# Gate rows by column matmuls and DMA, projections spread over slots, tiles finished at even steps

## The chip, the cores and the metric

One core of a Trainium2 chip. The metric is the device time of one execution in microseconds, median over runs. Where the times of two kernels are compared, the runs come from the same chip in the same rounds, unless the text says otherwise.

## The reference, cut to what matters

An adaptive layer norm, attention with 32 query heads over 8 groups of keys, a gated residual, a second norm, a spatial gating MLP, a second gated residual. Only the lines that the change touches:

```python
mod = (_silu(c) @ w_mod).reshape(c.shape[0], 6, 1, -1)
sa, ca, ga, sb, cb, gb = (mod[:, 0].copy(), ..., mod[:, 5].copy())   # cut
h = _layernorm(x, axis=-1) * (1 + ca) + sa
x = x + ga * _A_ref(h, A_k_cache, A_v_cache, A_wq, A_wo)             # ga: gate row 1
h = _layernorm(x, axis=-1) * (1 + cb) + sb
x = x + gb * _B_ref(h, B_w_in, B_w_sp, B_b_sp, B_w_out)              # gb: gate row 2
```

`x` is 2048 x 512, `c` one row of 512. `ga` and `gb` are needed as rows, the same on all 128 partitions.

## The kernel before

The attention runs as 128 iterations of 8 slots. A slot has a score pair (two 512-column matmuls into one of two `s_ps` buffers), one exponential on ScalarE, eight matmuls of probabilities by values of the iteration before (P.V), and whatever `fill` and `at` put there: query projections for later iterations, output projections, norms. `(it, i)` is iteration and slot; what `at` adds runs ahead of the slot's score pair, what `fill` adds runs after its P.V matmuls.

```python
def mod_part(i, wmod, w0, mc_ps):              # 16 matmuls of one column
    for dt in range(NDT):
        for kt in range(NDT):
            nc.tensor.matmul(mc_ps[:, i * NDT + dt : i * NDT + dt + 1],
                lhsT=wmod[:, kt, w0 + dt * P : w0 + (dt + 1) * P],
                rhs=sc_bf[:, kt : kt + 1], start=(kt == 0), stop=(kt == NDT - 1))

def ln1_turn(j0, n, xns):                      # transposes, then modulation; cut
    for half in range(2):
        t_ps = bank("misc")[:].bitcast(BF16).rearrange("p (k q) -> p k q", k=2)
        ...                                    # 2*n transposes into t_ps
        ...                                    # VectorE: two modulations out of t_ps

at(0, 3, first_turn)                           # turns tile 1
at(0, 6, lambda: ln1_turn(2, 2, first["x2"]))  # turns tiles 2 and 3: 8 transposes
...
fill[0, 4] = qproj(0, list(range(REP)), P, P)  # 16 projections of tile 1, then one copy
rest_q = qproj(0, [0, 1], 2 * P, 2 * P) + qproj(0, [2, 3], 2 * P, 2 * P)
fill[0, 7], fill[1, 0], fill[1, 1] = rest_q[0:5], rest_q[5:11], rest_q[11:16]
...
# the last column of the MLP: seven gate steps of 128 columns
for f in range(NFT):                           # NFT = 7
    spatial(last, yT, f, n_a, P, bias_by_pe=True)      # 16 matmuls, bias, VectorE multiply
    ...                                                # output matmuls of step f - 1
    if f % 2 == 1:
        finish_tile(last, f // 2, o2_last[f // 2])     # two VectorE operations, a store
```

`bank("misc")` hands out two PSUM banks (buffers that matmuls write their results into) in turn: the transposes of `ln1_turn`, the projections and the output projections all take theirs from these two. `bank("o_ps")` has two banks of its own.

## Time and profile before

| | before |
|---|---|
| time, first three runs | 1322.39 us (1322.29 to 1322.67) |
| span of the trace | 1320.8 us |
| TensorE busy | 1301.5 us (99%) |
| ScalarE busy | 1076.7 us (82%) |
| first score pair starts | 10.65 us |
| first slot with the next chunk's projections | its score pair at 31.42 us |
| last operation before the last store starts | 1316.08 us |

Read the table with the chain of waits in mind, the profile's list that goes back from the last instruction, at each step to what released it: TensorE carries 98% of it. Something is won only where TensorE has less to execute or waits less. The last three rows are landmarks.

### The profile page before, as it was taken

How to read it: one execution, taken by the hardware profiler on the slowest of the kernel's cores; microseconds unless marked ns; L12 is line 12 of the kernel's file. 1: busy time of each engine (PE TensorE's matmuls, PEld its weight loads, DVE VectorE, ACT ScalarE, POOL GpSimd, SP SyncE). 2: the span in 40 equal slices, each digit the busy share in tenths (PEclk: the TensorE clock that was granted, in tenths of full speed). 3: DMA queues.
4: the chain of work that ended last, by engine and by line, in shares of the span. 5: the costliest groups of instructions: out<-in, count | busy, mean ns of one | idle time of the engine just before them, and what ended most of it. 6: DMA issues, size and time to landing. Idle time of an engine off the chain costs nothing.

```text
span 1320.8 us, 27675 instructions
## 1 busy us (share of the span) xinstructions
PE 1301.5 (99%) x12130; PEld 858.3 (65%) x12335; DVE 473.4 (36%) x1166; ACT 1076.7 (82%) x1061; POOL 49.2 (4%) x92
## 2 busy tenths in 40 slices
PE   9999999999999999999999999999999999999998
PEld 5666666666666666666666666666666666644445
DVE  6532222222222222222222222222222566784444
ACT  7898999999999999999999999999999999650000
POOL 1200000000000000000000000000000000020000
PEclk9999999999999999999999999999999999999999
DMA  7541022102111122111210221021101111153300
GB/s 180 148 97 33 16 47 37 37 17 49 31 24 37 30 37 37 33 34 37 33 37 13 53 37 33 18 53 23 31 14 21 25 31 31 34 116 80 69 21 26
DMA packets 148720, 58.12 MB, mean 44 GB/s; under 512 B 138384, under 2 KB 144784, under 8 KB 148592
## 3 DMA queue, kind: packets, MB, share of 16 engines
q1 hardware_dynamic: 141792, 37.65, 15.4%
q0 software_dynamic: 4208, 16.39, 4.2%
q10 hardware_dynamic: 2592, 2.23, 0.5%
q8 instruction: 98, 1.61, 0.5%
q14 instruction: 30, 0.25, 0.1%
HBM read 21.37 MB, written 2.10 MB: 18 GB/s over the span
## 4 chain that ended last, share of the span: by engine, by line
PE 98%; issue 1%; DMA 0%; DVE 0%; ACT 0%; SPq 0%; DVEq 0%
PE s_ps L972 36%; PE o_ps L994 35%; PE misc L939 7%; PE misc L1345 7%; PE misc L1026 6%; PE s_ps L1191 2%; PE s_ps L1230 2%; PE o_ps L1366 1%; PE s_ps L1366 0%; DMA wmod_a<-in_w_mod_dram 0%; PE misc L1102 0%; DVE tmp L1378 0%; DVE yout L1379 0%; PE misc L849 0%; PE misc L1353 0%
## 5 line engine op out<-in xcount | busy, mean ns | idle before, releaser
L979 ACT ACTIVATE pT<-s_ps 128x1024 bf16<-128x1024 f32 x1024 | 1043.4, 1024 | 83.4 <-PE s_ps L972 8.5
L994 PEld LDWEIGHTS <-pT 128*128 128x128 bf16 x8192 | 548.5, 98 | 241.2
L994 PE MATMUL o_ps<-v,pT 128*128 128x129 bf16 x8192 | 631.4, 220 | 0.0
L972 PE MATMUL s_ps<-qT,kT 128*128 128x512 bf16 x2048 | 609.0, 379 | 10.0 <-ACT pT L979 0.2
L1005 DVE RECIPROCAL rall<-o_ps 128x2 f32<-128x2 f32 x256 | 43.7, 171 | 744.1 <-PE o_ps L994 744.0
L972 PEld LDWEIGHTS <-kT 128*128 128x128 bf16 x2048 | 199.3, 98 | 119.5 <-issue 1.0
L939 PE MATMUL misc<-hT,wq_g 128*128 128x512 bf16 (+2 forms) x466 | 166.4, 370 | 0.1
L1026 PE MATMUL misc<-wo_g,oT 128*128 128x512 bf16 x386 | 146.3, 379 | 0.0
L1006 DVE TENSOR_TENSOR onorm<-o_ps,rall 128x256 bf16<-128x256 f32 x256 | 108.6, 424 | 9.0 <-DVE rall L1005 0.3
L1345 PE MATMUL misc<-wsp,z 128*128 128x512 bf16 (+2 forms) x555 | 100.5, 336 | 0.6 <-issue 0.3
L950 DVE CAST qT<-misc 128x512 bf16<-128x512 f32 x127 | 86.4, 680 | 1.9 <-PE misc L939 1.6
L1345 PEld LDWEIGHTS <-z 128*128 128x128 bf16 x560 | 50.6, 98 | 48.5
L1039 DVE TENSOR_TENSOR xacc<-misc,xacc 128x512 f32<-128x512 f32 x112 | 76.2, 680 | 0.0
L939 PEld LDWEIGHTS <-wq_g 128*128 128x128 bf16 x528 | 50.5, 98 | 0.7
L1026 PEld LDWEIGHTS <-oT 128*128 128x128 bf16 x512 | 50.1, 98 | 0.8
L1360 DVE TENSOR_TENSOR gb<-misc,bsp_bc 128x512 bf16<-128x512 f32 (+1 forms) x28 | 18.4, 658 | 58.6 <-PE misc L1345 58.6
L1191 PE MATMUL s_ps<-win_sb,hT 128*128 128x448 bf16 x128 | 27.0, 352 | 0.1
L1201 ACT ACTIVATE z<-s_ps 128x896 bf16<-128x896 f32 x16 | 14.7, 917 | 14.9 <-PE s_ps L1191 14.9
L1230 PE MATMUL s_ps<-hT,win_sb 128*128 128x512 bf16 x109 | 24.3, 379 | 0.2
L1238 ACT ACTIVATE z1T<-s_ps 128x1024 bf16<-128x1024 f32 x14 | 14.3, 1023 | 10.1 <-PE s_ps L1230 9.1
L691 DVE BATCH_NORM_STATS2 bnst<-x_sb 128x6 f32<-128x512 bf16 x32 | 21.9, 683 | 1.3 <-DMA x_sb<-in_A_x_dram 0.8
L715 POOL DMA_DIRECT2D wq_g<-in_A_wq_dram x7 | 5.2, 750 | 420.9 <-PE misc L939 420.9
(87 smaller groups left out, 281.5 us busy)
## 6 DMA issues: line engine op xcount, KB each, us to landing
wq_g<-in_A_wq_dram POOLq DMA_DIRECT2D x7, 512.0 KB, 4.0
v<-in_A_v_cache_dram POOLq DMA_DIRECT2D x7, 512.0 KB, 7.3
wo_g<-in_A_wo_dram POOLq DMA_DIRECT2D x7, 512.0 KB, 4.7
oT<-onorm SPq DMA_TRANSPOSE x128, 2.4
wsp<-in_w_mod_dram POOLq DMA_DIRECT2D x1, 2048.0 KB, 11.1
out_dram<-yout ACTq DMA_DIRECT2D x16, 128.0 KB, 1.7
win_sb<-in_B_w_in_dram POOLq DMA_DIRECT2D x1, 1792.0 KB, 7.6
x_sb<-in_A_x_dram SPq DMA_DIRECT2D x3, 512.0 KB, 5.9
```

The source lines that it names most:

```text
L939: nc.tensor.matmul(ps[0][:, o0 : o0 + n], lhsT=wqs[g][:, dt, hh * DH : (hh + 1) * DH], rhs=hTs[ch][:, dt, c0 : c0 + n], start=(dt == 0), s ...
L950: nc.vector.tensor_copy(out=dst, in_=src)
L972: nc.tensor.matmul(s_ps[:, h * 512 : (h + 1) * 512].rearrange("p (r q) -> p r q", r=REP), lhsT=groups[g]["kT"][:, kt * P : (kt + 1) * P], ...
L979: nc.scalar.activation(out=pTs[u][:, 2 * i : 2 * i + 2, :], in_=s_ps[:].rearrange("p (k q) -> p k q", k=2), func=ACT.Exp, scale=inv_sqrt_dh,)
L994: nc.tensor.matmul(o_ps[:, hh % 2, 0 : DH + 1], lhsT=pTs[u][:, kt, hh * P : (hh + 1) * P], rhs=groups[g]["v1"][:, kt, 0 : DH + 1], start=( ...
L1005: nc.vector.reciprocal(out=rall[:, c0 : c0 + 2], in_=o_ps[:, :, DH])
L1006: nc.vector.tensor_tensor(out=onorms[u][:, hh - 1 : hh + 1, :], in0=o_ps[:, :, 0:DH], in1=rall[:, c0 : c0 + 2].unsqueeze(2).to_broadcast([ ...
L1026: nc.tensor.matmul(X_ps[:], lhsT=oTs[u][:, hh, :], rhs=groups[g]["wo"][:, hh, :], start=(hh == 0), stop=(hh == REP - 1),)
L1039: nc.vector.tensor_tensor(out=xaccs[j][:], in0=X_ps[:], in1=xaccs[j][:], op=ALU.add)
L1191: nc.tensor.matmul(ps[0][:, hf * 512 : hf * 512 + FC], lhsT=h2Ts[j // CT][:, dt, (j % CT) * P : (j % CT + 1) * P], rhs=win_sb[:, dt, FH + ...
L1230: nc.tensor.matmul(ps[0][:, k * 512 : (k + 1) * 512], lhsT=win_sb[:, dt, f * P : (f + 1) * P], rhs=h2Ts[2 * ch2 + k][:, dt, :], start=(dt ...
L1345: nc.tensor.matmul(g_ps[:, :n], lhsT=z2[:, st, f * P : (f + 1) * P], rhs=wsp[t][:, st, c0 : c0 + n], start=(st == 0), stop=(st == NT - 1 a ...
```

## The change

The intent has three parts. The gate rows are computed as columns (cheap one-column matmuls) and turned into rows by a trip through DRAM, in place of eight 512-column matmuls. The projections near the start are spread thinner, so that ScalarE should not wait for score pairs behind long runs of projections. And three of the last four tiles are finished one gate step earlier.

```diff
-    def mod_row(row_out, i, lhs):
-        mr_ps = bank("misc")
-        for kt in range(NDT):
-            nc.tensor.matmul(mr_ps[:], lhsT=lhs[kt][:], rhs=wmod_b[:, kt, ...], ...)   # cut
-        nc.vector.tensor_copy(out=row_out[:], in_=mr_ps[:])
+    def mod_rows():
+        mc_ps = bank("misc")
+        for i, row in enumerate((0, 3)):
+            mod_part(i, wmod_b, row * D, mc_ps)
+        for i, (part, rows) in enumerate(((2, ga_rows), (5, gb_rows))):
+            cols = slice(part * NDT, (part + 1) * NDT)
+            nc.vector.tensor_copy(out=modc[:, cols], in_=mc_ps[:, i * NDT : (i + 1) * NDT])
+            line = dram.tile([D], FP32, name=f"mod{part}")
+            nc.gpsimd.dma_start(out=line[:].rearrange("(dt p) -> p dt", p=P), in_=modc[:, cols])
+            nc.gpsimd.dma_start(out=rows[:], in_=line[:].partition_broadcast(P))
...
-    fill[0, 4] = qproj(0, list(range(REP)), P, P)
+    next_q = qproj(0, list(range(REP)), P, P)
+    fill[0, 4], fill[0, 5] = next_q[0:8], next_q[8:16]
     rest_q = qproj(0, [0, 1], 2 * P, 2 * P) + qproj(0, [2, 3], 2 * P, 2 * P)
-    fill[0, 7], fill[1, 0], fill[1, 1] = rest_q[0:5], rest_q[5:11], rest_q[11:16]
+    fill[0, 7] = rest_q[0:4]
+    for i in range(6):
+        fill[1, i] = rest_q[4 + 2 * i : 6 + 2 * i]
...
-    at(10, 4, lambda: mod_row(ga_rows, 2, rest_w["lhs"]))
-    at(11, 4, lambda: mod_row(gb_rows, 5, rest_w["lhs"]))
+    at(10, 4, mod_rows)
...
-        if f % 2 == 1:
+        if f % 2 == 0 and f < 2 * (CT - 1):
             finish_tile(last, f // 2, o2_last[f // 2])
```

(Also cut: the helper that made the broadcast weights for `mod_row`, and the DRAM pool.)

More of the change, by code (lines that the diff above doesn't have):

```diff
@@ L637 @@
     )
+    dram = fast.enter_context(tc.tile_pool(name="dram", bufs=1, space=bass.MemoryType.DRAM))
     res = fast.enter_context(tc.tile_pool(name="res", bufs=1))
@@ L1081, in ln2 @@
         at(it + 2, 5, third)
-    def mod_lhs():
-        lhs = []
-        for kt in range(NDT):
-            lhs_bc = res.tile([P, P], BF16, name=f"lhs_bc{kt}")
-            nc.vector.tensor_scalar_mul(
-                out=lhs_bc[:], in0=ones_bf[:], scalar1=sc[:, kt : kt + 1]
-            )
-            lhs.append(lhs_bc)
-        return lhs
     def mod_cols_b():
@@ L1097, in mod_cols_b @@
         mod_copy(3, mc_ps)
-    def mod_row(row_out, i, lhs):
-        mr_ps = bank("misc")
-        for kt in range(NDT):
-            nc.tensor.matmul(
-                mr_ps[:],
-                lhsT=lhs[kt][:],
-                rhs=wmod_b[:, kt, (i - 2) * D : (i - 1) * D],
-                start=(kt == 0),
-                stop=(kt == NDT - 1),
-            )
-        nc.vector.tensor_copy(out=row_out[:], in_=mr_ps[:])
+    def mod_rows():
[8 more added lines that the diff above has]
+            nc.gpsimd.dma_start(out=rows[:], in_=line[:].partition_broadcast(P))
     def load_wsp(tile_, t, st):
@@ L1149 @@
     ln1_at(3, (5, 1), (5, 5), (7, 4))
-    rest_w = {}
     at(2, 5, lambda: nc.gpsimd.dma_start(out=wmod_b, in_=wmod_dram[:, :, 2 * D : NMOD]))
     at(5, 5, lambda: nc.gpsimd.dma_start(out=win_sb[:], in_=win_dram))
-    at(8, 1, lambda: rest_w.update(lhs=mod_lhs()))
     at(9, 4, mod_cols_b)
-    at(10, 4, lambda: mod_row(ga_rows, 2, rest_w["lhs"]))
-    at(11, 4, lambda: mod_row(gb_rows, 5, rest_w["lhs"]))
+    at(10, 4, mod_rows)
     def set_fill(b):
```

## The prediction

> **What bounds the kernel now.** I read the page first, for the shares; then the chain of waits in order of time, which names the engine that time cannot be taken from; then the table of stretches and the timeline at the four places that the diff touches.
>
> ```profile
> PE 1301.5 (99%) x12130; PEld 858.3 (65%) x12335; DVE 473.4 (36%) x1166; ACT 1076.7 (82%) x1061; POOL 49.2 (4%) x92
> PE 98%; issue 1%; DMA 0%; DVE 0%; ACT 0%; SPq 0%; DVEq 0%
> ```
>
> TensorE is 98% of the chain that ended last, so a change counts only where it removes TensorE work, or a wait in front of TensorE. There is little to win from waits: 1% of 1320.8 us is 13 us, most of it before the first matmul and at the very end. Three small places are left, and the diff goes to each. The first is the gate rows. These are the pieces of the chain, and the same slots as stretches with TensorE's busy time in each:
>
> ```profile
> 94.12 0.78 PE misc L849 x32
> 103.73 0.86 PE misc L1102 x4
> 113.40 0.86 PE misc L1102 x4
> 92.86:93.96 1.10, 1.10 (x12) 1.00 0.00 0
> 93.96:94.76 0.80, 0.80 (x33) 1.00 0.00 0
> 103.56:104.43 0.87, 0.87 (x6) 1.00 0.00 0
> 113.23:114.10 0.87, 0.87 (x6) 1.00 0.09 19
> ```
>
> A plain slot of this stage (two score matmuls, eight P.V matmuls, one projection) takes 1.10 us, all of it TensorE. The two gate rows (line 1102) lengthen their slots by 0.87 us each. The 32 one-column matmuls that make the shift and scale columns of the second norm (line 849) lengthen theirs by 0.80. An exponential every 0.92 us (below) fits in 1.10 us, so nothing but TensorE paces these slots.
>
> The second place is the start, where ScalarE and TensorE take turns as the bound:
>
> ```profile
> 14.61 1.17 PE L939 MATMUL misc<-hT,wq_g 128*128 128x128 bf16 x16
> 15.62 0.59 PE L972 MATMUL s_ps<-qT,kT 128*128 128x512 bf16 x2
> 15.82 0.69 DVE L950 CAST qT<-misc 128x512 bf16<-128x512 f32 x1
> 16.05 0.90 PE L826 MATMUL misc<-ident,xn 128*128 128x128 bf16 x8
> 16.25 4.02 ACT L979 ACTIVATE pT<-s_ps 128x1024 bf16<-128x1024 f32 x4 [0.29 <-PE s_ps L972]
> 20.66 1.02 ACT L979 ACTIVATE pT<-s_ps 128x1024 bf16<-128x1024 f32 x1 [0.39 <-PE s_ps L972]
> 22.09 11.11 ACT L979 ACTIVATE pT<-s_ps 128x1024 bf16<-128x1024 f32 x12 [0.41 <-PE s_ps L972]
> ```
>
> The brackets are ScalarE's idle time: 0.29 us because sixteen projections sit in front of the score matmuls at 15.62, then 0.39 and 0.41 because of the five or six projections in each of the next slots. The eight transposes should last 0.45 us but end at 16.79: half of them need the bank that the copy of 15.82 still reads until 16.53.
>
> The third place is the end (chain of waits):
>
> ```profile
> 1313.25 0.70 DVE tmp L1378
> 1313.97 0.69 DVE yout L1379
> 1314.66 0.21 DVE yT L1361
> 1314.92 0.40 PE s_ps L1366
> ```
>
> VectorE finishes tile 2 while the last gate step is ready for it; TensorE waits for that step.
>
> **What the Trainium skill says.** "TensorE: Matmul & The Clock Gate", section "Back-to-back issue gap", gives about 60 cycles (a floor near 25 ns) for a matmul of 1 to 64 columns and 518 cycles for 512. This trace agrees: 0.78 us / 32 = 24 ns and 0.86 / 4 = 215 ns. Its sustained 131 ns at 512 columns is not what this kernel shows. Section "LDWEIGHTS" of that page gives 128 columns / 1.2 = 107 ns per load, the same for any moving size; here a load lasts 96 ns, yet 32 load-and-matmul pairs pass in 0.80 us, so the loads overlap. "Perfetto Trace Analysis", section "Matmuls", wants independent groups to rotate through PSUM banks so that evacuation overlaps; the wait at 16.5 is that rotation (two buffers of misc) running out. "DMA: Bandwidth & Descriptors", section "Anatomy of one DMA", puts the fixed cost of a transfer near 2.0 us; the GpSimd weight loads here land 4.0 to 7.3 us after issue.
>
> **The change, part by part.**
>
> Gate rows. Removed: two groups of four 512-column matmuls (2 x 0.87 = 1.74 us of path), four VectorE multiplications for the broadcast weights, two 0.68 us copies. Added: 32 one-column matmuls with the same helper and shapes as the columns at 94.12, so 0.80 us; two small copies (the trace has 0.15 us for 128x4); two writes of 512 floats to DRAM and two reads back over all partitions. All the TensorE part lies on the path: 0.80 - 1.74 = -0.94 us. The DMA part costs nothing if it lands before use:
>
> ```profile
> L1044 DVE TENSOR_TENSOR xacc<-xacc,ga_rows x16: 691/693/693, 1035.6 to 1159.8; 128x512 f32<-128x512 f32 x16
> ```
>
> The rows are made near 105 us and first read at 1035.6. GpSimd's next work after them is a weight load that it issues at 113.69 in this trace; two write-and-read pairs at an estimated 4 to 8 us (from the skill's 2 us each and the landings above) about fit before it, and being a few us late there harms nothing, as those weights are used a group later.
>
> The end. Tiles 0 to 2 are finished after steps 0, 2 and 4 in place of 1, 3 and 5. VectorE then has nothing in hand when step 6 arrives. The last bias matmul starts at 1314.04 and lasts 0.23, so the gate multiplication can start at about 1314.29, not 1314.58: the last output matmul, the two 0.69 us operations and the store all move by 0.3 us. Do the earlier finishes hurt? Each is 1.4 us of VectorE between steps 1.37 us apart. Step 3's multiplication would be ready at 1310.18 but comes at about 1310.7, and step 5's at about 1313.3 in place of 1312.92. Their readers in TensorE come one step later (1311.45 and 1314.19), so no wait. Sum: -0.3 us.
>
> The start. Rules that I took from the trace: an exponential starts 0.63 us after its score pair starts (10.65 to 11.28, 15.62 to 16.25), exponentials follow each other at 0.917 us ((4.69 - 1.02) / 4 over the first five), and a score pair can start 1.07 us after the exponential two earlier started (two buffers). With 0.43 us a score pair, 0.455 for eight P.V matmuls, 0.11 for a projection of 256 columns, these rules give every start of before to 0.03 us: 16.79, 18.50, 20.03, 21.46, 25.00, 31.42. Now the new order. Eight projections, pair at 15.15, eight projections to 16.06, the copy to 16.77: 0.25 later than now, because a score pair stands between the halves. The second half of the transposes waits for it, and the next score pair starts at 17.04 (now 16.79), its exponential at 17.67 (17.42). The pair that opens the second iteration needs that exponential: 17.67 + 1.07 = 18.74 (18.50). From there six slots have two projections each before their successors: the next pair starts 1.11 us on, at 19.85, and so on to about 25.4 for slot 6 (25.00). The seven slots after it pass at 0.885 while TensorE gains on ScalarE and at 0.917 after, 6.29 us: the first slot of the next projections comes at about 31.65 (31.42). So the ScalarE stalls of the three dense slots go, but the path loses 0.24 us, since the transposes' wait grew. From there on every slot of the stage carries more TensorE work, and the shift stays.
>
> Sum: -0.94 - 0.30 + 0.24 = -1.0 us; 1322.39 - 1.0 = 1321.4 us.
>
> **The rivals.** (1) The start gains as it was meant to. For it: three ScalarE stalls, 0.29 + 0.39 + 0.41 = 1.09 us, that the denser slots cause. Against it: from 18.5 us on TensorE has no gap in the timeline, and it executes the same matmuls in the new order. If half came through, the whole would be near 1320.6; if the start is neutral, 1321.15. (2) The one-column matmuls are bound by their weight loads, 32 x 96 ns = 3.1 us, which turns -0.94 into +1.3 and gives 1323.7. The stretch at 93.96 speaks plainly against it. (3) The trip through DRAM becomes a wait, or its 512 four-byte pieces hold up the transposes of the outputs that share the DMA engines. Those transposes land in 2.4 us and are read more than an iteration (8.8 us) later, so they would have to be four times slower. I expect 0; at worst one slot, +1 us. (4) The finish of tile 2 at step 4 delays step 5 more than I think; then the end gains 0 and the total is 1321.7.
>
> **Range and chances.** The two solid parts make -1.24; the start is uncertain by about 0.4 either way and the three runs of before spread over 0.4 us. I take 1321.4, with 1320.7 to 1322.1 for 8 in 10. Two per cent is 26 us, and no row that the diff touches is that large: faster 0.005, same 0.99, slower 0.005.
>
> **What would show it.** In the changed profile: no line-1102 pieces in the chain, two groups of 32 one-column matmuls of 0.8 us each and plain 1.10 us slots at the third place; gate rows written by DMA near 110 us with nobody waiting; the last gate multiplication right behind the last bias matmul (0.02 us rather than 0.31); the score pair after the eight transposes near 17.0 and the first slot of the next projections at 31.6. A later time of that slot than 32, or any wait of TensorE between 100 and 125 us, would make me wrong upwards; 31.2 or less would make rival 1 right.

## The result, and the profile after

| | before | after |
|---|---|---|
| median of six runs | 1322.62 us (1322.29 to 1323.04) | 1321.80 us (1321.61 to 1322.06) |
| first score pair starts | 10.65 | 10.65 |
| first slot with the next projections | 31.42 | 31.83 |
| last operation before the last store starts | 1316.08 | 1315.29 |

The ratio is 0.9994, 95% interval 0.9981 to 1.0007: the same by the 2% rule, and 0.8 us faster by medians. (A ratio here is the mean time of one kernel's fast runs over that of the other's of the same rounds, so not quite the ratio of the medians.) The interval holds 1.0, although no run of one kernel falls within the range of the other. The parts are therefore read from the traces.

The gate rows, in the chain of waits of the changed kernel (start, duration, work). The two groups of four 512-column matmuls are gone and a second group of 32 one-column matmuls stands at 104:

```profile
94.53 0.78 PE misc L850 x32
104.14 0.78 PE misc L850 x32
```

The same slots as stretches (duration, then TensorE busy). The slot with the second group takes 0.80 us more than a plain one, and the place of the second gate row is now a plain slot:

```profile
103.98:104.78 0.80, 0.80 (x33) 1.00 0.00 0
112.49:113.59 1.10, 1.10 (x13) 1.00 0.00 0
113.59:114.69 1.10, 1.10 (x13) 1.00 0.09 15
```

The DMA side, in GpSimd's timeline of the changed kernel. The bracket is GpSimd's idle time and what ended it:

```profile
105.55 0.76 POOL L1099 DMA_DIRECT2D mod<-modc  x1 [42.15 <-DVE modc L1097]
114.26 0.56 POOL L1100 DMA_DIRECT2D ga_rows<-mod  x1 [7.96 <-DMA mod<-modc]
126.45 0.55 POOL L1100 DMA_DIRECT2D gb_rows<-mod  x1 [10.88 <-DMA mod<-modc]
127.05 0.75 POOL L716 DMA_DIRECT2D wq_g<-in_A_wq_dram  x1
```

The two 2 KB writes keep GpSimd waiting 8 and 11 us, and the weight load behind them is issued at 127.05 in place of 113.69. No TensorE wait between 100 and 130 us follows from it in this trace, and the first gate row is first read at 1035.1. Another transfer does become slow: the transpose of outputs that SyncE issues at 118.7 lands 9.6 us later. In the seven traces of kernels with the new gate rows this one took 9.6 to 11.4 us; in the six traces without a DRAM trip it took 2.4. TensorE first reads its result at 132.0, 13.3 us after the issue, so nothing waits for it.

The start, in TensorE's timeline, with the new gap in the bracket:

```profile
16.05 0.39 PE L827 MATMUL misc<-ident,xn 128*128 128x128 bf16 x4
17.00 0.39 PE L827 MATMUL misc<-ident,xn 128*128 128x128 bf16 x4 [0.56 <-DVE qT L951]
17.22 1.03 PE L973 MATMUL s_ps<-qT,kT 128*128 128x512 bf16 x4
18.93 0.59 PE L973 MATMUL s_ps<-qT,kT 128*128 128x512 bf16 x2 [0.24 <-ACT pT L980]
```

and what ScalarE shows of it in the same stretch:

```profile
11.28 5.61 ACT L980 ACTIVATE pT<-s_ps 128x1024 bf16<-128x1024 f32 x6 [0.68 <-PE s_ps L973]
17.85 15.76 ACT L980 ACTIVATE pT<-s_ps 128x1024 bf16<-128x1024 f32 x16 [0.97 <-PE s_ps L973]
```

ScalarE's three stalls of 0.29, 0.39 and 0.41 us have become one of 0.97. From 17.85 on the listing merges sixteen exponentials into one piece, which looks like the success of the spreading. But the whole piece starts late, and its exponentials are (15.76 - 1.02) / 15 = 0.98 us apart on average, not 0.917: the six slots from 18.93 on are 1.10 us long, all of it TensorE's work, and ScalarE waits a little in each.

The end, in the chain of waits:

```profile
1313.59 0.17 PE misc L1344
1313.79 0.30 DVE yT L1352
1314.14 0.40 PE s_ps L1357
```

The multiplication of step 6 now begins 0.03 us after the bias matmul, not behind the finish of tile 2.

One trap on the page: TensorE's busy time rose from 1301.5 to 1311.8 us though it has less to do. The trace of before holds 12130 matmul records and the one of after 12359: records were missing in the first. The chain and the starts of slots do not depend on that.

### The profile page after: what moved, and what is told of

Same layout as the page of the kernel before. It is cut to its first block, busy times and chain, and to the rows that moved or that the text cites. A ratio compares the mean times of both kernels' runs of the same rounds, so it can differ in the third digit from the quotient of the medians.

```text
span 1320.0 us, 27930 instructions
## 1 busy us (share of the span) xinstructions
PE 1311.8 (99%) x12359; PEld 857.8 (65%) x12359; DVE 471.7 (36%) x1162; ACT 1077.1 (82%) x1061; POOL 51.8 (4%) x96
## 4 chain that ended last, share of the span: by engine, by line
PE 99%; DMA 0%; DVE 0%; ACT 0%; SPq 0%; issue 0%; DVEq 0%
PE o_ps L995 35%; PE s_ps L973 34%; PE misc L1027 8%; PE misc L940 8%; PE misc L1336 7%; PE s_ps L1182 2%; PE s_ps L1221 2%; PE o_ps L1357 1%; PE s_ps L1357 1%; DMA wmod_a<-in_w_mod_dram 0%; PE misc L850 0%; ACT pT L980 0%; PE misc L1344 0%; PE o_ps L781 0%; PE misc L827 0%; DVE qT L951 0%
## 5 line engine op out<-in xcount | busy, mean ns | idle before, releaser
L980 ACT ACTIVATE pT<-s_ps 128x1024 bf16<-128x1024 f32 x1024 | 1043.8, 1024 | 82.5 <-PE s_ps L973 7.4
L1027 PE MATMUL misc<-wo_g,oT 128*128 128x512 bf16 x512 | 194.2, 379 | 0.0
L940 PE MATMUL misc<-hT,wq_g 128*128 128x512 bf16 (+2 forms) x528 | 190.3, 371 | 0.0
L1229 ACT ACTIVATE z1T<-s_ps 128x1024 bf16<-128x1024 f32 x14 | 14.3, 1024 | 10.1 <-PE s_ps L1221 9.1
L1357 PE MATMUL o_ps<-wout_sb,yT 128*128 128x512 bf16 x84 | 20.1, 379 | 0.0
```

The source lines that it names most:

```text
L940: nc.tensor.matmul(ps[0][:, o0 : o0 + n], lhsT=wqs[g][:, dt, hh * DH : (hh + 1) * DH], rhs=hTs[ch][:, dt, c0 : c0 + n], start=(dt == 0), s ...
L980: nc.scalar.activation(out=pTs[u][:, 2 * i : 2 * i + 2, :], in_=s_ps[:].rearrange("p (k q) -> p k q", k=2), func=ACT.Exp, scale=inv_sqrt_dh,)
L1027: nc.tensor.matmul(X_ps[:], lhsT=oTs[u][:, hh, :], rhs=groups[g]["wo"][:, hh, :], start=(hh == 0), stop=(hh == REP - 1),)
L1357: nc.tensor.matmul(dst, lhsT=yT[:, f, jj * P : (jj + 1) * P], rhs=wout_sb[:, f, :], start=(f == 0), stop=(f == NFT - 1),)
```

## The experiments

All kernels gave correct results. "To the next projections" is the time from the first score pair to the score pair of the first slot with the next projections; "to the last operation" is the time from the first score pair to the start of the last VectorE operation. Both are differences of starts in one trace.

| run | time, median | before, same rounds | to the next projections | to the last operation |
|---|---|---|---|---|
| before | | | 20.77 | 1305.43 |
| after | 1321.80 | 1322.62 | 21.18 | 1304.64 |
| e1_rows | 1321.60 | 1322.49 | 20.77 | 1304.51 |
| e2_start | 1323.02 | 1322.49 | 21.18 | 1305.84 |
| e3_split | 1322.77 | 1322.49 | 21.19 | 1305.85 |
| e9_spread | 1322.41 | 1322.49 | 20.75 | 1305.41 |
| e4_end | 1322.15 | 1322.75 | 20.76 | 1305.15 |
| e6_rows_end | 1321.40 | 1322.75 | 20.76 | 1304.37 |
| e7_dma | 1322.60 | 1322.75 | 20.77 | 1305.43 |
| e5_after_bank | 1321.54 | 1322.75 | 20.63 | 1304.10 |
| e10_bank | 1322.40 | 1322.42 | 20.58 | 1305.23 |
| e8_best | 1321.48 | 1322.42 | 20.45 | 1303.91 |
| e11_best_again | 1320.94 | 1322.56 | 20.46 | 1303.91 |
| e12_rows_end_again | 1321.35 | 1322.56 | 20.76 | 1304.55 |

The first score pair itself came between 10.10 and 10.99 us in these traces, and the stretch from the last operation's start to the end of the span took 4.56 to 4.93 us, over kernels that share that code. This is as large as what is being measured, so the last two columns carry the verdicts, and the times are a check on their sum. Each row is one trace.

The traces hold all 1024 score pairs, so the changed kernel can be compared with before slot by slot. Slots differ by more than 0.02 us at three places only: from slot 4 of the first iteration to slot 2 of the third (together +0.41 us) and at the two old places of the gate rows (-0.06 and -0.86, together -0.92). The other -0.28 us comes after the last score pair.

**e1_rows: the gate rows alone.** The kernel after with the start and the end of before:

```diff
-    fill[0, 4], fill[0, 5] = next_q[0:8], next_q[8:16]
+    fill[0, 4] = qproj(0, list(range(REP)), P, P)
+    # rest_q and finish_tile as in the kernel before
```

> The kernel before with the new gate rows alone. My theory (three independent terms that add): two groups of 32 one-column matmuls of 0.80 us in place of one of 0.80 and two of 0.87, so -0.94 us in time and in the trace; the start unchanged (score pair after the eight transposes at 16.79, first slot of the next projections at 31.42). Rival (the round trip through DRAM costs something on the path): less than -0.6, with a TensorE gap between 100 and 130 us.

Measured: 0.92 us less to the last operation, 0.89 by medians; the start unchanged at 20.77. The DRAM trip costs nothing on the path of this trace; e6 and e12 below show that it is not always so.

**e2_start, e3_split, e9_spread: the start, whole and in its two halves.** The edits against the kernel before:

```diff
 e3_split:
-    fill[0, 4] = qproj(0, list(range(REP)), P, P)
+    next_q = qproj(0, list(range(REP)), P, P)
+    fill[0, 4], fill[0, 5] = next_q[0:8], next_q[8:16]
 e9_spread:
-    fill[0, 7], fill[1, 0], fill[1, 1] = rest_q[0:5], rest_q[5:11], rest_q[11:16]
+    fill[0, 7] = rest_q[0:4]
+    for i in range(6):
+        fill[1, i] = rest_q[4 + 2 * i : 6 + 2 * i]
 e2_start: both
```

> The kernel before with both edits of the start alone. My theory: the start loses what the two traces differ by there, 31.83 - 31.42 = +0.41 us. Rival (the spreading itself gains as meant, and the loss comes from elsewhere): 0 or faster.

> The kernel before with only the sixteen projections of the second tile split over slots 4 and 5. My theory: the split alone makes the loss, as it puts the copy behind one more score pair and so the second half of the transposes: copy from 16.25, score pair at 17.22, second iteration's first pair at 18.93, first slot of the next projections at about 31.83, time +0.41. Rival (the loss comes from the later, two-by-two spreading): +0.0 to +0.1.

> The kernel before with only the last sixteen projections spread (4, then two in each of six slots). My theory: neutral; TensorE has one projection less before 18.50 and idles 0.11 us there, and wins it back in ScalarE-paced slots later, so the first slot of the next projections stays at 31.42 within 0.05 and the time within 0.1. The intention of the change: the two stalls of ScalarE of 0.39 and 0.41 go and 0.3 us or more is won. Rival of e3: +0.3 or more.

Measured to the last operation: +0.41 for both, +0.42 for the split alone, -0.02 for the spreading alone. The times agree in sign and roughly in size (+0.53, +0.28, -0.08). The split alone makes the loss; the spreading is neutral and takes neither a gain nor a loss through. The chain of waits of e3_split shows the loss being made: eight projections, a score pair, eight projections, the copy, and only then the second half of the transposes:

```profile
14.88 0.43 PE s_ps L972 x2
15.31 0.46 PE misc L939 x8
15.80 0.70 DVE qT L950
16.54 0.38 PE misc L826 x4
17.39 1.03 ACT pT L979
18.47 0.59 PE s_ps L972 x2
```

The last two lines carry the loss on: the late score pair makes its exponential late, and the second iteration's first pair (18.47) needs the buffer that this exponential reads.

**e4_end: the end alone.**

```diff
-        if f % 2 == 1:
+        if f % 2 == 0 and f < 2 * (CT - 1):
```

> The kernel before with the finishes of tiles 0 to 2 after steps 0, 2 and 4 alone. My theory: -0.3 us, all of it between the last bias matmul and the last output matmul, with no new TensorE gap in steps 1 to 6. Rival (the earlier finishes delay odd steps): 0 to -0.15, with a gap before step 4, 5 or 6.

Measured: -0.28 to the last operation (-0.60 by medians, beside a scatter of 1321.99 to 1322.68 within its own five runs). No step waits for an early finish: the chain goes from bias matmul to output matmul to the next step at steps 5 and 6 as in the changed kernel.

**e6_rows_end and e12_rows_end_again: gate rows and end, start of before.** The kernel after with the two `fill` edits undone; the second is the same kernel run again.

> The changed kernel with the start of before. My theory: the terms add, -0.94 - 0.30 = -1.24 us from before and 0.4 us less than the changed kernel. Rival (the terms overlap): not below the changed kernel.

> The kernel of e6_rows_end once more: 20.77 us from the first pair to the next projections, -1.2 us from before to the last output operation counted from the first pair (the first trace had one stray slot of 1.25 us in place of 1.10 at 114 us and showed -1.06; if that is chance it is gone), time 1.2 below before.

Measured: the times are 1.35 and 1.21 us below before, as expected from the sum, where the changed kernel was 0.82 below in its own rounds. To the last operation the two traces show -1.06 and -0.88, less than -1.20. The difference is one slot in each, the same one: its score pairs are 1.25 and 1.44 us apart in place of 1.10. The expectation of e12 that this was chance is refuted. With its excess of 0.15 and 0.34 us taken off, both traces come to -1.21 and -1.22. The chain of waits of the second run shows what the slot waits for (its first piece is cut to the window asked for):

```profile
112.99 1.07 PE s_ps L973
114.08 1.03 ACT pT L980
115.11 0.04 issue
115.15 0.59 PE s_ps L973 x2
```

The score pair at 115.15 waits for the buffer that the exponential of 114.08 reads, and that exponential starts 1.47 us after its own score pair (112.61) in place of 0.63; in e6 it starts 1.28 us after it (113.12 to 114.40). With slots of 1.10 us and the prediction's 1.07 us from an exponential to the pair two later, a lag of up to 2 x 1.10 - 1.07 = 1.13 us costs nothing, and 1.28 and 1.47 cost 0.15 and 0.34, as seen. This one exponential, of iteration 11, slot 4, lags in all seven traces with the new gate rows (0.67 in the changed kernel, 0.91 in e1, 1.05 and 1.13 in e8 and e11, 1.15 in e5) and stands at 0.63 in the other seven. It starts within 0.7 us before GpSimd issues the first read, so about when the first DRAM write lands. The new gate rows are therefore not always free: they cost 0.15 and 0.34 us in two of seven traces. Why the exponential is late is left open.

**e7_dma: the DMA part alone.** Added to the kernel before, at the same place of the program, with the old gate rows moved to iterations 17 and 18 so that they overwrite what it brings:

```diff
+    def extra_dma():
+        for part, rows in ((3, ga_rows), (4, gb_rows)):
+            cols = slice(part * NDT, (part + 1) * NDT)
+            line = dram.tile([D], FP32, name=f"mod{part}")
+            nc.gpsimd.dma_start(out=line[:].rearrange("(dt p) -> p dt", p=P), in_=modc[:, cols])
+            nc.gpsimd.dma_start(out=rows[:], in_=line[:].partition_broadcast(P))
+    at(10, 4, extra_dma)
-    at(10, 4, ...mod_row ga)   -    at(11, 4, ...mod_row gb)
+    at(17, 4, ...mod_row ga)   +    at(18, 4, ...mod_row gb)
```

> The kernel before with the DMA part of the new gate rows added (two writes of 512 floats in four-byte pieces, two broadcast reads) at the same place, and its own gate rows moved six or seven iterations later so that they overwrite what those reads bring. My theory: the DMA part is off the path, 0 within 0.1 us, though each write takes about 10 us to land. Rival: +0.2 us or more, or waits of TensorE for transposed outputs between 105 and 130 us.

Measured: 0.00 to the last operation, -0.15 by medians. The transfers are free here, and slow: GpSimd waited 9.06 and 11.98 us for the two writes, and the transpose of outputs issued at 108.6 landed after 11.2 us in place of 2.4, so the transfers alone slow it. One thing differs from the change: the columns are ready sooner here, and the first write is issued at 95.53 in place of 105.55. No exponential lags in this trace, so it does not test the lag that e6 and e12 show.

**e5_after_bank and e10_bank: the second half of the transposes in another bank.** In the kernel after and in the kernel before:

```diff
-            t_ps = bank("misc")[:].bitcast(BF16).rearrange("p (k q) -> p k q", k=2)
+            name = "o_ps" if j0 == 2 and half == 1 else "misc"
+            t_ps = bank(name)[:].bitcast(BF16).rearrange("p (k q) -> p k q", k=2)
```

> The changed kernel with the second half of the eight transposes in a bank of the output tiles, which nothing uses then, so that they need not wait for the copy. My theory (the bank is what the transposes wait for): no TensorE gap at 16.4 to 17.0, score pair near 16.5 rather than 17.22, first slot of the next projections at about 31.3 rather than 31.83, time 0.5 us below the changed kernel, 1.3 below before. Rival (ScalarE's rate or VectorE's modulation after the copy sets the pace anyway): 0 to -0.15 from the changed kernel.

> The kernel before with the second half of the eight transposes in the free output bank and nothing else. My theory: the wait of 0.30 us for the copy goes, the second iteration opens 0.2 us earlier as ScalarE then becomes the bound, and the first slot of the next projections comes at about 20.57 us from the first score pair in place of 20.77. Rival: the wait is hidden by ScalarE's own pace, 20.77.

Measured in the kernel after: 0.55 us less to the next projections (20.63 against 21.18), 0.54 less to the last operation; the wait is the bank's. By time it lies 1.21 below before, where 1.3 was expected. What sets the start there is VectorE's modulation after the late copy, from the chain of waits of e5_after_bank:

```profile
16.48 0.69 DVE qT L952
17.17 1.28 DVE hT L809 x4
18.49 0.27 PE misc L941
18.76 0.43 PE s_ps L974 x2
```

In the kernel before: 0.19 us less to the next projections and 0.20 to the last operation, and there ScalarE becomes the bound, as expected (the chain now has the exponential of 16.11 just before the pair of 17.19). The median did not show it, 1322.40 against 1322.42. At 0.2 us it is below what five runs resolve.

**e8_best and e11_best_again: a version from these findings.** Gate rows and end as in the change, the sixteen projections back in one slot, the other bank, and the last sixteen spread:

```diff
     fill[0, 4] = qproj(0, list(range(REP)), P, P)
-    fill[0, 7], fill[1, 0], fill[1, 1] = rest_q[0:5], rest_q[5:11], rest_q[11:16]
+    fill[0, 7] = rest_q[0:5]
+    for i in range(6):
+        fill[1, i] = rest_q[5 + 2 * i : 7 + 2 * i]
```

> The changed kernel with the sixteen projections of the second tile back in one slot, the second half of the eight transposes in the free output bank, and the last sixteen spread as 5, 2, 2, 2, 2, 2, 1. By the rules of the prediction the second iteration opens 0.2 us earlier than before and the first slot of the next projections comes 0.3 us earlier, counted from the first score pair (20.77 before, so about 20.45). With rows and end: -0.92 - 0.28 - 0.3 = -1.5 us from before, 0.7 below the changed kernel. Rival (ScalarE's exponentials or VectorE's modulation set the pace there): 20.6 or later, no better than the changed kernel with the start of before.

> The kernel of e8_best once more, beside e12 on the same chip. Its trace of the first run confirmed -1.5 us from the first score pair on (20.45 to the next projections), but its first pair came at 10.99 us, later than in any other trace (10.20 to 10.87), and the time showed only -0.9. If that late start is chance (when the first weight load lands), the trace again shows 20.45 and -1.5 counted from the first pair, the first pair lies anywhere between 10.2 and 11.0, and the time is 0.3 us below e12. If the late start belongs to this kernel, the first pair is again at 10.9 or later and the time is not below e12.

Measured: -1.52 us to the last operation in both traces, 20.45 and 20.46 to the next projections. The first series showed only 0.94 us by medians, with the first score pair of its trace at 10.99; the second showed 1.62 (1320.94 us, ratio 0.9989, interval 0.9975 to 1.0002) with the first pair at 10.39. The late start was chance, or at least did not belong to the kernel. Taken together it is the fastest version that I found, below both the kernel before and the change, though by its own interval no ratio here is clear of 1.0. The spreading that was neutral in e9 is worth about 0.13 us here (20.58 in e10 to 20.45). The slots show why: seven slots before the next projections pass at ScalarE's 0.92 us in e10 and three in e8, the other four at TensorE's 0.885, and four times 0.03 us is the gain. e9 wins the same four slots, but the slot before its pair at 18.62, which waits for an exponential anyway, hands on one projection of 0.11 us; the two nearly cancel. By this account the other bank is not needed for the gain; a run with this spreading in the old bank was not made.

## Why the prediction was right

**The bound.** Right: TensorE's own work and the waits in front of it were all that moved the time. e7 added four transfers and GpSimd waits of 9 and 12 us, and TensorE lost nothing by them.

**The gate rows, -0.94.** Right: -0.92 in e1. The price of one group of 32, read from a place where the same helper already ran, held at 0.80; the old rows were worth 0.86 each in the slots, not 0.87. The rival that each matmul would pay for its weight load (+1.3) is refuted.

**The end, -0.3.** Right: -0.28 in e4, and the shifts of the odd steps stayed harmless. They were smaller than worked out: counted from its bias matmul, the multiplication of step 3 came 0.17 us later than before (0.5 expected), that of step 5 0.29 later (0.4 expected).

**The start, +0.24.** Right in sign and mechanism, too small: +0.41. The mis-sized term is the start of the copy. The prediction put it at the end of the sixteenth projection's slot, 16.06, and the copy's end at 16.77; the copy began at 16.25 and ended at about 16.95. The last matmul's result comes 0.2 us after its slot ends: the trace of before showed this (score pair issued at 15.62, copy from 15.82), and the prediction read the end 16.53 from that copy but not the delay. These 0.18 us went through the rest of the working unchanged: 17.22 for 17.04, 18.93 for 18.74, 31.83 for 31.65. A slip in the working is hidden in the last figure: 18.74 + 6 x 1.11 + 6.29 is 31.69. The slots took 1.10 each, so the slip and the rounding about cancelled.

**The DMA times.** Off in size, harmless: a write and read pair was put at 4 to 8 us and took about 13 (105.55 until the read of 114.26 landed, 4.6 us later) and about 16. The landings that the estimate took, 4.0 to 7.3 us, also left out two weight loads of GpSimd in the same trace, 7.6 and 11.1 us. GpSimd's next weight load was expected to fit and came 13 us later; no slot after it is longer than before, so the slack absorbed it, as the prediction had said it would.

**The rival of the DRAM trip.** Not refuted, but harmless in the changed kernel, partly by luck. The prediction said that the transposes would have to be four times slower to matter; one was, 9.6 us for 2.4 (11.4 in e6). It did not matter because its reader comes 13.3 us after the issue, not 8.8. The late exponential was not foreseen; it cost the changed kernel nothing at a lag of 0.67, and e6 and e12 0.15 and 0.34 us, within the "at worst one slot" of the prediction.

**The sum.** -0.92 - 0.28 + 0.41 = -0.79 us, and the landmarks of the changed kernel's trace give -0.79 (1304.64 against 1305.43); the medians give -0.82. Predicted was -1.0; the difference is the copy's 0.18 and 0.02 each from the rows and the end. The rival that the start gains as it was meant to is refuted by e2, e3 and e9.

## What to carry to other kernels

Before spreading work thinner, look at what waits for its last piece: here the copy after the sixteenth projection freed a bank for the next transposes, and moving that piece behind one more score pair cost 0.42 us, while the stalls of ScalarE that the spreading removed were worth nothing in e9 (-0.02), as TensorE had no gap behind them. Take durations for added operations from a place in the same trace where the same helper runs, and count the delay from a matmul's slot to the first reader of its result. When the start of the kernel varies more than the effect, measure between landmarks inside one trace, and compare slot by slot: a stray wait in one slot can hide in a difference of landmarks.

## What the Trainium skill lacked or had wrong

- "TensorE: Matmul & The Clock Gate", "Back-to-back issue gap": its sustained 131 ns for 512 columns does not hold here, 0.86 us / 4 = 215 ns; the table of cycles (518) and the floor near 25 ns for one column do (0.78 us / 32 = 24 ns).
- "DMA: Bandwidth & Descriptors", "Anatomy of one DMA": a fixed cost near 2.0 us plus bytes over bandwidth is far below a 2 KB write to DRAM in 512 four-byte pieces: GpSimd waited 8.0 to 12.0 us for one. (The four bytes are the access pattern's; the trace of the changed kernel records sixteen packets of 128 bytes for the first write, between 106.9 and 107.3, and the read behind it was issued at 114.26.) The page has no figure for such a transfer. That the four-byte pieces are the cause was not tested: no run wrote the same 2 KB in one piece.
- No page that I read has how much the time of a kernel's first work varies: the first score pair came between 10.10 and 10.99 us over fourteen traces.
- No page that I read has a figure for what a small DRAM write does to its neighbours: a transpose from SBUF to SBUF beside it landed in 9.6 to 11.4 us in place of 2.4, and one exponential near its landing started 0.67 to 1.47 us after its score pair in place of 0.63, in all seven traces of kernels with the new gate rows.
